# Top-k attention and a dropless expert layer on one core: three experts' rows of the first batch are filled up to whole blocks with empty rows, and 27 blocks instead of 26 are dealt during attention

## The chip, the cores and the metric

The kernel runs on one core of one Trainium2 chip. The metric is the device time of one execution in microseconds (us). Three timed executions of the kernel before gave 1338.06, 1338.33 and 1339.21 us, so the median is 1338.33 us.

## The reference

The first half is attention with a top-k mask, the second an expert layer in which each row goes to one expert only. Cut to what matters:

```python
# q, k, v: (8 batches, 8 heads, 576, 64)
scores = (q @ k^T) / 8
kth = the 32nd largest score of each query row
scores = where(scores >= kth, scores, -1e9)
attn_out = softmax(scores) @ v
x = attn_out as 4608 rows of 512          # 576 rows from each batch
logits = x @ w_gate                       # 8 experts
expert_idx = argmax(logits)
gate_w = softmax(logits)[expert_idx]
for e in range(8):                        # rows of expert e
    y[rows] = relu(x[rows] @ w1[e]) @ w2[e]   # 512 -> 1024 -> 512
return gate_w * y
```

All data is 32-bit floating point. How many rows each expert gets is known only when the kernel runs.

## The kernel before, in words

**Attention.** The work is cut into 144 groups, 18 for each of the 8 batches. A group is two tiles of 128 query rows; a unit is two heads of one batch, and nine groups make two units. One pass of the main loop (`loop`, L1123 on, `i` is the group) issues, for its group: on VectorE a fold of the next group's scores (L306, L308, later L314, L316), a search of the 32 largest values (MAX8 and MATCH_REPLACE8 on L345, L354, L362); on ScalarE `low` (L371), the depth below the threshold (L387) and the exponential (L404); on GpSimd the subtraction between those two (L396); on TensorE the scores of a group four ahead (L292), transposes (L415, L427, L429) and, once per unit, the product with v (L450). The orders of TensorE, ScalarE and VectorE are written out by hand; the queues of SP and GpSimd are laid out by the framework, apart from GpSimd instructions that are chained to each other.

**Dealing blocks.** When the last unit of a batch ends (`ending`, L1012 on), the batch's 576 rows are scattered to a DRAM buffer `x_rows` (L567, five indirect DMAs on GpSimd's queue), where every expert has a range of its own of CAP = 4736 rows. `run` holds the next free row of each expert. Then `table` (L597 to L654, fifteen small VectorE instructions on one partition for a batch) lists full blocks: blocks of 128 rows that no later row can change. How many are listed after each batch is fixed when the program is built, in `new_of`: 0, 4, 4, 5, 4, 5, 4 for the batches 0 to 6, 26 in all. Where `new_of` is 0, no table is made.

**Blocks in the shadow of attention.** A block (`block`, L879 on) loads 257 KB of rows (L749) and 4 MB of weights (L741, L743; two buffers), transposes the rows (L788), multiplies by w1 (L893), applies relu (L898), multiplies by w2 (L910), scales (L919) and puts its rows out with an indirect DMA (L808). Its TensorE work is handed out in 16 pieces: eight of four matmuls on L893, eight of one on L910 (in the trace each matmul is two instructions). A planner in `loop` spends a credit: it grows in each group by `rate` for each of its two tiles, and `rate` is set at group 13 of each batch b from 1 on to `new_of[b - 1] * 16 / 36`. So 4 blocks are spread over the 18 groups that follow at 3.56 pieces a group, 5 blocks at 4.44. In the last five groups of the last batch the credit is spread so that KEEP = 48 pieces, three blocks, are left over. These fill TensorE while the last batch is being finished.

**The end.** After the last batch, `counted` counts each expert's full blocks (a rest of over 64 rows is filled up and counts as full) and its halves (a rest of 1 to 64 rows). A first table gives SURE = 2 blocks, then `end_table` (L669 to L736) gives the rest: HALVES = 4 slots in which a full block and a half of the same expert go through the weights together (`long_block`, 192 rows), and PLAIN = 4 slots of plain blocks. `fill_up` (L582) writes 128 empty rows behind each expert's last row. An empty row has a scale of 0 and an output row number past the end, so that nothing is written for it; the rows come from the tile `blank`. What does not fit the slots is counted in `rest_i`, and a branch behind the main part works it off; another branch repeats everything exactly if a search was in doubt. After attention 3 kept, 2 sure, 4 long and 4 plain blocks follow.

At the start of the program SP's queue loads the first units and then writes one block of empty rows (L942), to which unused slots point.

Of the kernel before, what the change touches and what calls it, by code (L numbers as in the profile page):

```python
# [9 lines left out]
F32 = mybir.dt.float32  # L10
I32 = mybir.dt.int32
AF = mybir.ActivationFunctionType
ALU = mybir.AluOpType
# [24 lines left out]
def _inner(ap: bass.AP, n: int) -> bass.AP:  # L38
    return _ins(ap, len(ap.ap), n)
# [3 lines left out]
def kernel(  # L43
# [47 lines left out]
    nc = tc.nc  # L91
    B, U, P, _ = qk.shape
    N, Dm = out.shape
    S = N // B
    E = moe_w_gate.shape[1]
# [4 lines left out]
    ST = S - SM  # L100
# [7 lines left out]
    FT = F // P  # L108
    XW = Dm + 2
    EB = N // P  # L110
    NSLOT = EB + E - 1
    CAP = N + P
    EMPTY = E * CAP // P
# [1 line left out]
    assert N % P == 0 and TOP_K == 32 and DT == U and P == 2 * D  # L115
    scale = float(D) ** -0.5
    sure = [max(0, -((E * (P - 1) - S * (b + 1)) // P)) for b in range(B - 1)]
    upto_of = [max(0, (S * (b + 1) - E * ST) // P - 1) for b in range(B - 1)]
    upto_of = [max(a, c) if b else 0 for b, (a, c) in enumerate(zip(sure, upto_of))]
    new_of = [b - a for a, b in zip([0] + upto_of, upto_of)]  # L120
    assert all(n >= b - a for n, a, b in zip(new_of, [0] + sure, sure))
    LAST = NSLOT - sure[-1]
    HALVES = E // 2
    SURE = 2
    PLAIN = EB - upto_of[-1] - HALVES - SURE
    LONG = P + ST
    assert PLAIN >= 0 and (N - E * (P - 1) + P - 1) // P - upto_of[-1] >= SURE
    assert LAST - SURE + HALVES <= NSLOT and PLAIN + HALVES <= NSLOT

    k = SimpleNamespace()  # L130
# [25 lines left out]
    const = ctx.enter_context(tc.tile_pool(name="const", bufs=1))  # L156
# [5 lines left out]
    x_rows = dram.tile([(EMPTY + 1) * P, XW], F32, name="x_rows")  # L162
# [16 lines left out]
    for odd in range(2):  # L179
        for h in range(2):  # L180
            r = slice(h * D, (h + 1) * D)
# [16 lines left out]
    e_at = iota_f("e_at", [P, E], [[CAP, E]])  # L198
# [18 lines left out]
    run = const.tile([P, E], F32, name="run")  # L217
    nc.vector.tensor_copy(run, e_at)
    rest_i = const.tile([1, 1], I32, name="rest_i")
    rare = const.tile([1, 1], F32, name="rare")  # L220
    slot_last = const.tile([1, 2, NSLOT], I32, name="slot_last")
    slot_long = slot_last[:, 0, NSLOT - 3 * E:].rearrange("o (i e) -> o i e", i=3)
    assert LAST - SURE <= NSLOT - 3 * E
    done = const.tile([1, E], F32, name="done")
    nc.vector.tensor_scalar_mul(done, e_at[0:1, :], 1.0 / P)
    slot_max = const.tile([1, 2], F32, name="slot_max")
    nc.vector.memset(slot_max[:, 0:1], float(E - 1))
    nc.vector.memset(slot_max[:, 1:2], float(EMPTY))
    upto_all = const.tile([1, E + 1], F32, name="upto_all")
# [7 lines left out]
    blank = const.tile([P, XW], F32, name="blank")  # L237
# [323 lines left out]
    def scattering(r, x):  # L561

        mine = []

        def scatter(i):
            rows_i = slice(0, P if i < NC else ST)
            put = nc.gpsimd.indirect_dma_start(  # L567
                out=x_rows[:, :], out_offset=bass.IndirectOffsetOnAxis(ap=r.posi[rows_i, i:i + 1], axis=0),
                in_=x[rows_i, i, :], in_offset=None,
            ).ins  # L570
            if not k.exact:
                tc.add_manual_dep(put, k.last_pool.name, AFTER)
                for other in mine:
                    tc.declare_no_dep(put, other, reason="the rows of one batch go to different places")
                for other in fetched:
                    tc.declare_no_dep(put, other, reason="new rows go behind all full blocks")
                mine.append(put)
                scattered.append(put)

        return [lambda i=i: scatter(i) for i in range(KC)]  # L580
# [16 lines left out]
    def table(slot_i, n, last, riding=None):  # L597

        sm = k.small
        full = sm.tile([1, E], F32, name="full")  # L600
        ci = sm.tile([1, E], I32, name="ci")
        left = sm.tile([1, E], F32, name="left")
        past = sm.tile([1, NSLOT, E], F32, name="past", bufs=1)
        slot_f = sm.tile([1, 2, NSLOT], F32, name="slot_f", bufs=1)
        upto, step = upto_all, step_all

        def steps():
            if last:
                nc.vector.tensor_scalar_add(full, run[0:1, :], float(P - 1))
                yield  # L610
            nc.vector.tensor_copy(ci, full if last else run[0:1, :])
            yield
            nc.vector.tensor_single_scalar(ci, ci, 7, op=ALU.arith_shift_right)
            yield
            nc.vector.tensor_copy(full, ci)
            yield
            if riding is not None:
                nc.vector.tensor_tensor(full, full, riding, op=ALU.subtract)
                nc.vector.tensor_tensor(full, full, done, op=ALU.max)
                yield  # L620
            nc.vector.tensor_tensor(left, full, done, op=ALU.subtract)
            yield
            nc.vector.tensor_tensor_scan(upto[:, 1:], ones[0:1, 0:E], left, 0.0, op0=ALU.mult, op1=ALU.add)
            yield
            nc.vector.tensor_tensor(step[:, 0:E - 1], done[:, 1:E], full[:, 0:E - 1], op=ALU.subtract)
            yield
            nc.vector.tensor_tensor(
                past[:, 0:n, :], _inner(slots[:, 0:n], E), _ins(upto[:, 1:], 1, n), op=ALU.is_ge
            )
            yield  # L630
            nc.vector.tensor_reduce(slot_f[:, 0, 0:n], past[:, 0:n, :], axis=AX.X, op=ALU.add)
            yield
            nc.vector.tensor_tensor(past[:, 0:n, :], past[:, 0:n, :], _ins(step[:, :], 1, n), op=ALU.mult)
            yield
            nc.vector.tensor_reduce(slot_f[:, 1, 0:n], past[:, 0:n, :], axis=AX.X, op=ALU.add)
            yield
            nc.vector.scalar_tensor_tensor(
                out=slot_f[:, 1, 0:n], in0=slot_f[:, 1, 0:n], scalar=done[:, 0:1], in1=slots[:, 0:n],
                op0=ALU.add, op1=ALU.add,
            )  # L640
            yield
            nc.vector.tensor_tensor(slot_i[:, :, 0:n], slot_f[:, :, 0:n], _inner(slot_max[:, :], n), op=ALU.min)
            yield
            if last:
                nc.vector.tensor_copy(rest_i, upto[:, E:])
            else:
                nc.vector.tensor_scalar_min(upto, upto, float(n))
                yield
                nc.vector.tensor_tensor(left, upto[:, 1:], upto[:, 0:E], op=ALU.subtract)
                yield  # L650
                nc.vector.tensor_tensor(done, done, left, op=ALU.add)
                yield

        return steps()  # L654

    def counted():

# [11 lines left out]
    def end_table(slot_i, slot_l, n, half, full):  # L669
# [16 lines left out]
            v.tensor_scalar(to, to, what[:, 0:1], None, ALU.add)  # L686

        def steps():
            v.tensor_tensor_scan(hupto[:, 1:], ones[0:1, 0:E], half, 0.0, op0=ALU.mult, op1=ALU.add)
            v.tensor_tensor(left, full, done, op=ALU.subtract)  # L690
            v.tensor_scalar(take, hupto[:, 1:], float(HALVES), None, ALU.is_le)
            v.tensor_tensor(take, take, half, op=ALU.mult)
            v.tensor_tensor(take, take, left, op=ALU.min)
# [16 lines left out]
                out=slot_f[:, 1, 0:m], in0=slot_f[:, 1, 0:m], scalar=done[:, 0:1], in1=at[:, 0:m],  # L710
                op0=ALU.add, op1=ALU.add,
            )
            v.tensor_tensor(slot_i[:, :, 0:n], slot_f[:, :, 0:n], _inner(slot_max[:, :], n), op=ALU.min)
            yield
            v.tensor_tensor(past[:, 0:E, :], _inner(slots[:, 0:E], E), _ins(hupto[:, 1:], 1, E), op=ALU.is_ge)
            v.tensor_reduce(long_f[:, 0, :], past[:, 0:E, :], axis=AX.X, op=ALU.add)
# [220 lines left out]
    with fast:  # L937
        units = [(b, u) for b in range(B) for u in range(U)]
        unit.append(load_unit(*units[1]))
        for n in unit:  # L940
            load_values(n)
        nc.sync.dma_start(x_rows[EMPTY * P:(EMPTY + 1) * P, :], blank)  # L942

        work = [(b, g) for b in range(B) for u in range(0, U, 2) for g in groups(u)]
        per_batch = len(work) // B
# [66 lines left out]
        def ending(b, u):  # L1012
# [48 lines left out]
            yield "pool"  # L1061
            through(steps)
            scatters.extend(scattering(r, x))
            if b == B - 1:
                scatter(KC)
                slot_i = k.small.tile([1, 2, NSLOT], I32, name="slot_i")
                half, full = counted()
                through(table(slot_i, SURE, False, half))
                firsts = [(slot_i[0:1, 0, j:j + 1], slot_i[0:1, 1, j:j + 1]) for j in range(SURE)]
                ready = load_rows(SimpleNamespace(), firsts[0][1], True)  # L1070
# [15 lines left out]
            if b == B - 1:  # L1086
                spare.extend(coming[PLAIN:])
                del coming[PLAIN:]
                longs = [[slot_long[0:1, i, j:j + 1] for i in range(3)] for j in range(E)]
                spare.extend((expert, half) for expert, half, _ in longs[HALVES:])  # L1090
                coming[0:0] = [(expert, [full, half]) for expert, half, full in longs[:HALVES]]
                assert len(loaded) == 2 and not waiting
                fill_up()
                coming[0:0] = [(firsts[0][0], ready)] + [(expert, (piece,)) for expert, piece in firsts[1:]]
                scatter(0)
# [126 lines left out]
    with ExitStack() as outer:  # L1222
# [10 lines left out]
        with ExitStack() as st:  # L1233
# [44 lines left out]
                    put()  # L1278
                nc.vector.tensor_scalar_add(ids, ids, S)
            fill_up()  # L1280
            slot_i = slot_last
            for _ in table(slot_i, NSLOT, True):
                pass
            nc.sync.dma_start(slot_d.rearrange("(a n) o -> o a n", a=2), slot_i)
# [53 lines left out]
```

## Time and profile before

| what | value |
|---|---|
| median of three timed executions | 1338.33 us (1338.06 to 1339.21) |
| the profiled execution's own time | 1339.03 us |
| its span, first to last instruction | 1337.4 us |
| TensorE matmul busy | 1189.3 us (89%) |
| VectorE busy | 1076.6 us (81%), 4629 instructions |
| ScalarE busy | 930.8 us (70%) |
| GpSimd busy | 661.9 us (49%) |
| weights loaded | 72 DMAs of 2 MB: 36 blocks |
| mean granted TensorE clock | 0.955 |

The span has two stages that overlap a little. Up to about 1073 us attention runs, and VectorE is busy almost without a gap; blocks are added on TensorE from 367 us on. From then on VectorE has nearly nothing to do, and TensorE works through the remaining blocks. Two things help in reading the rows. A busy share near 100% says that an engine has no gaps, not that its instructions run at their best: VectorE instructions of one line have different lengths in this trace. And a group of the attention loop can be told in the trace by the first fold, L306, which comes once in each of the 144 groups; the time from one to the next is the length of a group, about 7 us.

### The profile page before, as it was taken

The numbers are of one execution on the slowest core, as the hardware profiler recorded it, in microseconds if no ns is written. First come the engines' busy times: TensorE is split into PE (matmuls) and PEld (weight loads), VectorE is DVE, ScalarE is ACT, GpSimd is POOL, SyncE is SP. The second block draws the span as 40 slices with busy tenths as digits, with TensorE's granted clock in tenths as the row PEclk, the third lists the DMA queues.
The fourth block names the chain that finished last, engine by engine and source line by source line (L and its number), as shares of the span: only waits on it lengthen the run. The fifth ranks groups of instructions, "written<-read, shape, count | busy, mean of one in ns | idle before, by whom it ended". The sixth has DMA issues, their size and how long they took to land. (4 is left out here: it accounts for less than half of the span.)

```text
span 1337.4 us, 24295 instructions
## 1 busy us (share of the span) xinstructions
PE 1189.3 (89%) x7570; PEld 831.4 (62%) x7570; DVE 1076.6 (81%) x4629; ACT 930.8 (70%) x2125; POOL 661.9 (49%) x805
## 2 busy tenths in 40 slices
PE   5667766766799999999999999999999999999995
PEld 3344443444466766676677666666677667699973
DVE  7999999999999999999999999999999932000000
ACT  4788788887888888888787888887778851111110
POOL 3454547555755665567555756475547642000000
PEclk9788788888899999999999999999999999999998
DMA  2000001001384348435855294329452739946790
GB/s 84 30 29 30 30 29 65 29 29 38 122 305 168 108 164 288 160 110 175 297 208 179 74 350 170 118 76 372 171 204 87 283 116 332 369 146 219 290 342 18
DMA packets 95563, 214.36 MB, mean 160 GB/s; under 512 B 4926, under 2 KB 25662, under 8 KB 95424
## 3 DMA queue, kind: packets, MB, share of 16 engines
q1 hardware_dynamic: 88800, 192.45, 40.8%
q0 software_dynamic: 6336, 19.97, 4.2%
q8 instruction: 61, 1.00, 0.3%
q14 instruction: 78, 0.64, 0.2%
q10 hardware_dynamic: 288, 0.30, 0.1%
HBM read 191.42 MB, written 21.80 MB: 159 GB/s over the span
## 5 line engine op out<-in xcount | busy, mean ns | idle before, releaser
L396 POOL TENSOR_TENSOR w<-s,w 128x576 f32<-128x576 f32 x288 | 410.2, 1444 | 418.4 <-ACT w L387 418.4
L893 PE MATMUL ph<-xTs,w 128*128 128x128 f32 x2048 | 250.2, 276 | 5.9 <-ACT xTs L790 5.9
L893 PEld LDWEIGHTS ph<-xTs,w 128*128 128x128 f32 x2048 | 239.1, 192 | 21.9 <-issue 14.6
L910 PE MATMUL py<-w,hT 128*128 128x512 f32 x512 | 236.2, 597 | 0.0
L404 ACT ACTIVATE w<-w,nbias 128x576 f32<-128x576 f32 x288 | 224.1, 792 | 3.0 <-POOL w L396 2.0
L292 PE MATMUL sc<-qkb 64*128 64x288 f32 (+1 forms) x1280 | 206.0, 473 | 9.5 <-ACT s L299 5.1
L387 ACT ACTIVATE w<-s,low 128x576 f32<-128x576 f32 x288 | 207.6, 768 | 4.7
L415 PE MATMUL wTm<-turn,w 128*128 128x128 f32 x1152 | 170.1, 287 | 32.0 <-ACT xl L468 21.4
L415 PEld LDWEIGHTS wTm<-turn,w 128*128 128x128 f32 x1152 | 132.0, 145 | 92.5 <-issue 34.4
L299 ACT COPY s<-sc 128x576 f32<-128x576 f32 x288 | 168.9, 640 | 10.4 <-PE sc L292 10.4
L1217 DVE CAST any_i<-pd 1x1 int32<-1x1 f32 x1 | 0.1, 145 | 207.9 <-PE pd L1215 207.9
L422 ACT COPY wT<-wTm 128x512 f32<-128x512 f32 x256 | 139.2, 604 | 39.3 <-PE wTm L415 39.2
L354 DVE MAX8 tops<-scr 128x8 f32<-128x168 f32 x576 | 162.8, 317 | 0.0
L450 PE MATMUL po<-wT,vb 128*64 128x288 f32 x1024 | 154.9, 450 | 0.4 <-ACT wTt L437 0.4
L354 DVE MAX8 tops<-few 128x8 f32<-128x144 f32 (+1 forms) x576 | 154.4, 300 | 0.0
L292 PEld LDWEIGHTS sc<-qkb 64*128 64x128 f32 (+1 forms) x1280 | 110.1, 195 | 65.4 <-issue 25.6
L910 PEld LDWEIGHTS py<-w,hT 128*128 128x128 f32 x512 | 90.7, 190 | 90.4 <-issue 89.2
L808 POOL DMA_INDIRECT out_dram<-y,xg x40 | 42.6, 1066 | 189.8 <-ACT y L869 82.5
L345 DVE MAX8 few<-l 128x8 f32<-128x288 f32 x288 | 127.3, 442 | 0.0
L450 PEld LDWEIGHTS po<-wT,vb 128*64 128x64 f32 x1024 | 74.2, 150 | 77.3 <-issue 26.0
L306 DVE TENSOR_TENSOR h<-s 128x576 f32<-128x576 f32 x144 | 114.8, 797 | 3.9 <-ACT s L299 3.7
L308 DVE TENSOR_TENSOR l<-s 128x576 f32<-128x576 f32 x144 | 108.0, 750 | 0.0
(175 smaller groups left out, 1649.8 us busy)
## 6 DMA issues: line engine op xcount, KB each, us to landing
w<-in_moe_w_dram SPq DMA_DIRECT2D x72, 2048.0 KB, 8.6
qkb<-in_qk_dram SPq DMA_DIRECT2D x31, 608.0 KB, 5.8
vb<-in_v_dram SPq DMA_DIRECT2D x32, 320.0 KB, 3.1
xg<-x_rows SPq DMA_DIRECT2D x36, 257.0 KB, 10.6
x_rows<-blank SPq DMA_DIRECT2D x5, 257.0 KB
x_rows<-blank POOLq DMA_DIRECT2D x4, 257.0 KB, 8.2
x_rows<-x,posi POOLq DMA_INDIRECT x40, 3.1
out_dram<-y,xg POOLq DMA_INDIRECT x40, 4.5
```

The lines of the kernel that those rows point to most:

```text
L292: nc.tensor.matmul(ps[rows, j, 0:HF], n.q[d, cols], n.k[d, keys], start=True, stop=True)
L299: lambda m=m, ps=ps: nc.scalar.copy(s[:, m, :, :], ps[:, :, 0:HF]) for m, ps in enumerate(got)
L345: nc.vector.max(out=f.few[:, m, QF + 8 * j:QF + 8 * j + 8], in_=away)
L354: nc.vector.max(out=tops[:, m, r * 8:(r + 1) * 8], in_=src[m])
L387: nc.scalar.activation(w[:, m, :], s[:, m, :, :].rearrange("p j k -> p (j k)"), AF.Relu, scale=-STEEP, bias=low[:, m:m + 1],)
L396: k.last_pool = in_turn(nc.gpsimd.tensor_tensor(w[:, m, :], s[:, m, :, :].rearrange("p j k -> p (j k)"), w[:, m, :], op=ALU.subtract)).ins
L404: nc.scalar.activation(w[:, m, :], w[:, m, :], AF.Exp, scale=scale, bias=nbias[:, m:m + 1], accum_out=n.z[:, c:c + 1])
L415: nc.tensor.transpose(pm[:, c * P:(c + 1) * P], w[:, m, first:first + P], ident)
L422: nc.scalar.copy(wT[:, :, m, q], pm4)
L450: nc.tensor.matmul(po[r, 0:HF], n.v[:, c, r], rhs, start=(c == 0), stop=(c == KC - 1))
L893: nc.tensor.matmul(ph[:, f, :], n.w1[:, 0, dt, fc * P:(fc + 1) * P], n.xT[:, dt, :], start=(dt == 0), stop=(dt == DT - 1),)
L910: nc.tensor.matmul(py, hT[:, f, :], n.w2[:, 0, f, :], start=(f == 0), stop=(f == FT - 1))
```

## The change

The rows of batch 0 no longer wait for batch 1. Behind batch 0, a new function picks the three experts with most rows (at least as many as the third largest count) and moves their `run` on to 128, so that each of them has one full block:

```python
def filled_up():
    most, few = k.small.tile([P, E], F32, name="left"), k.small.tile([P, E], F32, name="full")
    nc.vector.tensor_tensor(few, run, e_at, op=ALU.subtract)
    nc.vector.max(out=most, in_=few)
    nc.vector.tensor_scalar(few, few, most[:, SOON - 1:SOON], float(P), ALU.is_ge, ALU.mult)
    nc.vector.tensor_tensor(few, few, e_at, op=ALU.add)
    nc.vector.tensor_tensor(run, run, few, op=ALU.max)
```

The rows between the batch's own and 128 are empty ones, which the start of the program writes at the head of each expert's range. The dealing changes to 3, 2, 4, 5, 4, 5, 4 blocks, 27 in all, so that a table is made behind batch 0 too and the first blocks are handed out from group 31 on (batch 1, group 13) instead of group 49. At the end, `end_table` turns a half whose expert has no full block left to go with it into a plain block. The diff, without the changes that only resize tables or move a tile:

```diff
+    SOON = 3
-    upto_of = [max(0, (S * (b + 1) - E * ST) // P - 1) for b in range(B - 1)]
-    upto_of = [max(a, c) if b else 0 for b, (a, c) in enumerate(zip(sure, upto_of))]
+    upto_of = [(S * (b + 1) - E * ST) // P for b in range(B - 1)]
+    upto_of = [max(a, c) if b else SOON for b, (a, c) in enumerate(zip(sure, upto_of))]
-    LAST = NSLOT - sure[-1]
+    LAST = NSLOT + SOON - sure[-1]
-    PLAIN = EB - upto_of[-1] - HALVES - SURE
+    PLAIN = EB - upto_of[-1] - HALVES - SURE + 1
...
         def steps():
+            v.tensor_tensor(left, full, done, op=ALU.subtract)
+            v.tensor_tensor(some, half, left, op=ALU.subtract)
+            v.tensor_scalar_max(some, some, 0.0)
+            v.tensor_tensor(half, half, some, op=ALU.subtract)
+            v.tensor_tensor(full, full, some, op=ALU.add)
+            v.tensor_tensor(left, left, some, op=ALU.add)
+            yield
             v.tensor_tensor_scan(hupto[:, 1:], ones[0:1, 0:E], half, 0.0, op0=ALU.mult, op1=ALU.add)
-            v.tensor_tensor(left, full, done, op=ALU.subtract)
...
-        nc.sync.dma_start(x_rows[EMPTY * P:(EMPTY + 1) * P, :], blank)
+        for r in [e * CAP for e in range(E)] + [EMPTY * P]:
+            nc.sync.dma_start(x_rows[r:r + P, :], blank)
...
             through(steps)
             scatters.extend(scattering(r, x))
+            if b == 0:
+                filled_up()
```

PLAIN stays 4 (36 - 26 - 4 - 2 before, 36 - 27 - 4 - 2 + 1 after); the last listing grows from 17 to 20 slots, and the three more go to the branch that works off what does not fit. SURE, HALVES, KEEP and the planner are as before.

More of the change, by code (lines that the diff above doesn't have):

```diff
@@ L117 @@
     sure = [max(0, -((E * (P - 1) - S * (b + 1)) // P)) for b in range(B - 1)]
-    upto_of = [max(0, (S * (b + 1) - E * ST) // P - 1) for b in range(B - 1)]
-    upto_of = [max(a, c) if b else 0 for b, (a, c) in enumerate(zip(sure, upto_of))]
+    upto_of = [(S * (b + 1) - E * ST) // P for b in range(B - 1)]
+    upto_of = [max(a, c) if b else SOON for b, (a, c) in enumerate(zip(sure, upto_of))]
     new_of = [b - a for a, b in zip([0] + upto_of, upto_of)]
     assert all(n >= b - a for n, a, b in zip(new_of, [0] + sure, sure))
-    LAST = NSLOT - sure[-1]
+    LAST = NSLOT + SOON - sure[-1]
     HALVES = E // 2
     SURE = 2
-    PLAIN = EB - upto_of[-1] - HALVES - SURE
+    PLAIN = EB - upto_of[-1] - HALVES - SURE + 1
     LONG = P + ST
-    assert PLAIN >= 0 and (N - E * (P - 1) + P - 1) // P - upto_of[-1] >= SURE
+    assert PLAIN >= 0 and E == 8 and SOON < E
     assert LAST - SURE + HALVES <= NSLOT and PLAIN + HALVES <= NSLOT
@@ L219 @@
     rest_i = const.tile([1, 1], I32, name="rest_i")
[L220 to L223, printed above, removed]
+    slot_last = const.tile([1, 2, NSLOT + SOON], I32, name="slot_last")
+    slot_long = slot_last[:, 0, NSLOT + SOON - 3 * E:].rearrange("o (i e) -> o i e", i=3)
+    assert LAST - SURE <= NSLOT + SOON - 3 * E
     done = const.tile([1, E], F32, name="done")
     nc.vector.tensor_scalar_mul(done, e_at[0:1, :], 1.0 / P)
-    slot_max = const.tile([1, 2], F32, name="slot_max")
+    slot_max = const.tile([1, 3], F32, name="slot_max")
+    rare = slot_max[:, 2:3]
     nc.vector.memset(slot_max[:, 0:1], float(E - 1))
@@ L641, in steps @@
             yield
-            nc.vector.tensor_tensor(slot_i[:, :, 0:n], slot_f[:, :, 0:n], _inner(slot_max[:, :], n), op=ALU.min)
+            nc.vector.tensor_tensor(slot_i[:, :, 0:n], slot_f[:, :, 0:n], _inner(slot_max[:, 0:2], n), op=ALU.min)
             yield
@@ L712, in steps @@
             )
-            v.tensor_tensor(slot_i[:, :, 0:n], slot_f[:, :, 0:n], _inner(slot_max[:, :], n), op=ALU.min)
+            v.tensor_tensor(slot_i[:, :, 0:n], slot_f[:, :, 0:n], _inner(slot_max[:, 0:2], n), op=ALU.min)
             yield
@@ L1091, in ending @@
                 coming[0:0] = [(expert, [full, half]) for expert, half, full in longs[:HALVES]]
-                assert len(loaded) == 2 and not waiting
+                assert len(loaded) == 2
                 fill_up()
@@ L1280 @@
             fill_up()
-            slot_i = slot_last
+            slot_i = slot_last[:, :, 0:NSLOT]
             for _ in table(slot_i, NSLOT, True):
```

## The prediction

> **What bounds the kernel now.** First the page's 40 slices of 33.4 us, to see which engine is full where.
>
> ```profile
> PE   5667766766799999999999999999999999999995
> DVE  7999999999999999999999999999999932000000
> PEclk9788788888899999999999999999999999999998
> ```
>
> VectorE (DVE) is full until slice 32, some 1073 us, TensorE (PE) from slice 11 to the end. So there are three stages: VectorE alone, both, TensorE alone. Next I cut the span where blocks arrive, 18 groups to a row (by the first folds, L306; the first block matmul is near 367.5), and read the busy times.
>
> ```profile
> core 0: us, PE busy (x) PEld busy (x) DVE busy (x) ACT busy (x) POOL busy (x), PEclk, DMA share, GB/s
> 109.70:238.30 128.60, 90.64 (x538) 54.20 (x536) 128.00 (x557) 105.23 (x246) 74.58 (x93) 0.85 0.12 40
> 238.30:367.50 129.20, 92.15 (x554) 55.91 (x552) 129.20 (x572) 104.93 (x246) 74.40 (x93) 0.86 0.17 55
> 367.50:498.00 130.50, 126.21 (x856) 87.79 (x854) 130.50 (x573) 112.20 (x258) 78.45 (x96) 1.00 0.52 181
> 498.00:630.40 132.40, 129.12 (x876) 89.35 (x874) 132.06 (x572) 113.54 (x264) 80.94 (x97) 1.00 0.51 182
> 630.40:773.10 142.70, 140.99 (x951) 98.30 (x948) 139.34 (x573) 114.03 (x265) 87.63 (x98) 1.00 0.57 201
> 773.10:907.60 134.50, 131.22 (x887) 90.60 (x887) 133.37 (x572) 115.24 (x265) 82.52 (x97) 1.00 0.51 179
> 907.60:1050.30 142.70, 140.99 (x951) 98.33 (x948) 139.32 (x573) 114.05 (x264) 87.59 (x98) 1.00 0.55 196
> 1072.80:1137.00 64.20, 61.16 (x362) 43.52 (x362) 19.76 (x111) 21.54 (x51) 20.27 (x27) 0.97 0.71 232
> ```
>
> I call the rows 0, 1, A, B, C, D, E. Rows 0 and 1 have no block: 18 groups take 129 us, VectorE without a gap. Row A carries 4 blocks (the same cut for L893 and L910 has 256 and 62 instructions, that is 32 + 31 of 64 pieces) and takes only 1.3 us more. B and D also carry 4 and take 3.2 and 5.3 us more, C and E carry 5 and take 13.5 us more. **Four blocks to 18 groups are nearly free, a fifth is not.** The last row is the end of attention: TensorE is busy 61 of 64 us there. The end of the whole span is blocks in a row; on GpSimd the last two output DMAs, one a block, are 14.0 us apart:
>
> ```profile
> 1308.94 0.97 POOL L808 DMA_INDIRECT out_dram<-y,xg  x1 [13.48 <-ACT y L919]
> 1322.95 0.97 POOL L808 DMA_INDIRECT out_dram<-y,xg  x1 [13.04 <-ACT y L919]
> ```
>
> **What becomes of the blocks.** I worked the planner's rule through by hand, group by group. Before: 64, 64, 80, 64, 80 pieces from groups 49, 67, 85, 103, 121, then 16 more. After: 48 from group 31, 32 from group 49, and from group 67 on the same 64, 80, 64, 80, 16, group for group, with 49 pieces left after the loop both times. Then 3 kept, 2 sure, 4 long, 4 plain. So the end, and rows B to E, have the same plan; the 27th block is done in attention. What differs is rows 0, 1 and A: 0, 0, 4 blocks become 0, 3, 2.
>
> Does the data fit the slots? I counted the experts' rows from the reference's inputs. Batch 0 gives 103, 79, 74, 60, 96, 61, 55, 48; experts 0, 1 and 4 are filled up with 25 + 49 + 32 = 106 empty rows. The deals of 3, 2, 4, 5, 4, 5, 4 then all find full blocks. At the end 36 full blocks and 5 halves stand where 36 and 4 stood; one half (expert 1) has no partner, becomes a plain block, and 27 + 2 + 4 + 4 = 37 slots hold all. Nothing goes to the branch behind.
>
> **Part by part.**
>
> *A table behind batch 0.* Fifteen small instructions, one at a time between the search's. In batch 2 the groups that hold one start at 316.94, 324.81 and end at 332.23; the same two groups of batch 1, without one, run 188.98, 195.90, 203.04. 15.29 less 14.06 is **+1.23 us**, on VectorE and so on the path. Bounds: 15 x 0.15 (a row such as L615) = 2.3 above; 0.6 below, if half of it goes into gaps.
>
> *`filled_up`.* Five dependent instructions of 128x8 on VectorE behind a search. Four of their kind, L514 to L520 on 128x40, start at 1098.67 and end at 1099.33: 0.165 each, so **+0.8 us**. Below: 5 x 0.08 (1.23 / 15) = 0.4. Above: one of them meets GpSimd's L396, as L613 does here, 1.21 for 0.17 us:
>
> ```profile
> 321.17 0.17 DVE L613 TENSOR_SCALAR ci<-ci 1x8 int32<-1x8 int32 x1
> ...
> 450.54 1.21 DVE L613 TENSOR_SCALAR ci<-ci 1x8 int32<-1x8 int32 x1
> ```
>
> ```profile
> 448.93 2.79 POOL L396 TENSOR_TENSOR w<-s,w 128x576 f32<-128x576 f32 x2 [3.96 <-ACT w L387]
> ```
>
> so 1.9 us. I take 0.8, as L396 ends 3 us ahead of the end of a group in row 0 (190.19 + 2.84 for a group from 188.98 to 195.90). The Trainium skill (GPSIMD Engine Reference, 8. Key points) says that GpSimd shares SBUF interfaces with VectorE, against VectorE instructions with two SBUF inputs or in a 2-port mode; by it three of the five could meet GpSimd, 3 us, but only if they fall beside it.
>
> *Three blocks in row 1.* By A's row, which is 4 blocks in the same cold start, between 0 and 1.3; I take **+0.3**. Upper bound, if row 1 behaves like D: 5.3 x 3/4 = 4.0.
>
> *Two blocks in A instead of four.* A's largest excess is L613's 1.04 us above, in a group with TensorE full. With half of the pieces I take that it goes, **-1.0**; bounds -1.3 and +1.4 (D's 5.3 x 2/4 - 1.3).
>
> *B to E.* Same plan, entered with less behind: 0, at best B becomes A, -1.9.
>
> *Eight more writes of empty rows at the start.* 8 x 0.36 us (L942) of SP's time from 9.35 us on and 2.06 MB, at 209 to 345 GB/s as in the first microseconds some 6 to 10 us. SP's next DMA is a qkb load at 22.47 us, whose first matmul is at 56.74. So 0; were the queue held 30 us longer, VectorE would wait. The scatters of batch 0 come near 200 us.
>
> *`end_table`.* Five more links, some 1.0 us, between 1106.6 and 1114 us. `fill_up`'s writes behind it wait for the scatters until 1117.3 anyway, SP's next weight load is at 1123.7, and TensorE has the kept blocks: 0, at most 1.0. The 27th block's DMAs (one L749, L741, L743 on SP, one L808 of 1.04 us on GpSimd) fall into rows 1 and A, where the DMA share was 0.17 and 0.52: 0.
>
> Sum: 1.23 + 0.8 + 0.3 - 1.0 = **+1.3 us**. On the profiled execution's own 1339.03 us (span 1337.4 and 1.6 around it) that is 1340.3. It lies 0.7 above the median, so the prediction is 1338.33 + 1.3 = **1339.6 us**.
>
> The clock is a rule against the change. Rows 0 and 1 have 0.85 and 0.86, row A has 1.00; row 1 after lies between. The Trainium skill (TensorE: Matmul & The Clock Gate, What's actually happening) has the array at half rate after an idle window of about 3.4 us, and at full rate only after a busy one. Spread thinner, by that rule, three blocks of 14.0 us at 0.85 would make 92 + 49 = 141 us of TensorE work in 129, +12 us; by row A, where 63 pieces raised the clock at once, nothing.
>
> **The rivals.**
>
> 1. *The blocks push GpSimd's subtraction into the second fold* (slower). In row 0 L396 ends 1.7 us before L314 starts (193.03, 194.69). Once ScalarE is over 1.7 us late they meet: in row C L314 and L316 at 698.66 take 1.40 and 1.66 for 0.44 and 0.45 us, +2.2 a time. For it: B and D, same plan, 3.2 and 5.3. Against it: A. Price: 1.23 + 0.8 + 4.0 + 1.4 = +7.4, 1345.7 us; half of it 1342.
>
> 2. *A cleaner entry* (faster). B behaves as A and A as row 1: 1.23 + 0.8 - 1.3 - 1.9 = -1.2, 1337.2 us. It would take another 1.5 us from C to pass the measurement's limit.
>
> 3. *The change doesn't do what it says:* the 27th block isn't absorbed and is left at the end, 14.0 + 2.0, 1354.3 us. The worked plan speaks against it.
>
> **How the numbers follow.** About 0.2% (2.7 us, so under 1335.7 or over 1341.0) is what a measurement can tell from no change. The forecast has 0.55, rival 2 0.17, rival 1 0.25, rival 3 0.03. The forecast's own range is 1338.4 to 1341.0. Rival 2 lies in no change but for 0.06 that passes 1335.7. Of rival 1 about 0.22 lies over 1341, with rival 3 0.25. So faster 0.06, no change 0.69, slower 0.25. The range cuts 0.06 below 1336.6 and some 0.14 above 1344.0.
>
> **What would show it.** In the profile after: L893 starts near 238 us; L613 occurs eight times, the first near 193 us; VectorE's groups 18 by 18 take about 130.6 (row 0, with table and `filled_up`), 129.5, 129.5, and then B to E unchanged; 74 weight loads, and from the last fold to the end the same time. Wrong if L314 and L316 grow beside L396 in rows 1 and A, if TensorE's clock stays at 0.85 there, if VectorE waits for s before 60 us, or if more than 49 pieces are left after the loop.

## The result, and the profile after

The changed kernel takes 1341.18 us (median of 11; 1339.65 to 1343.12) where the kernel before took 1338.92 us in the same series (median of 11; 1337.48 to 1339.44). The ratio is 1.0020 with a 95% interval of 1.0011 to 1.0029: 2.3 us slower (1.5 to 3.9), at the edge of what was called no change. The forecast was 1.3 us. The profiled execution took 1340.06 us, with a span of 1338.4, only 1.0 us over the span of before. Why one execution shows less than the medians is part of what follows.

The first of the views shown of before, the 40 slices of the page, now of the kernel after:

```profile
PE   5667767898988889999999999999999999999995
DVE  7999999999999999999999999999999942000000
PEclk9788887999998989999999999999999999999998
```

The blocks begin four slices earlier: counted from 0, TensorE is near 80 or 90% from slice 7 on, where it was at 60 or 70. Its clock rises with them, but falls back in slices 12 and 14, in the stretch with two blocks. VectorE stays full. Then the same rows of 18 groups, cut at the first folds as before, in the order 0, 1, A, B, C, D, E, end of attention:

```profile
core 0: us, PE busy (x) PEld busy (x) DVE busy (x) ACT busy (x) POOL busy (x), PEclk, DMA share, GB/s
108.90:240.50 131.60, 94.99 (x544) 57.08 (x542) 131.37 (x578) 104.99 (x246) 75.41 (x93) 0.82 0.17 54
240.50:370.80 130.30, 118.88 (x800) 79.64 (x798) 130.30 (x573) 110.99 (x257) 79.43 (x95) 0.98 0.41 145
370.80:501.10 130.30, 108.07 (x698) 70.08 (x695) 129.50 (x572) 108.93 (x254) 76.67 (x95) 0.93 0.31 109
501.10:632.60 131.50, 128.24 (x870) 89.00 (x868) 131.16 (x572) 112.64 (x259) 80.78 (x97) 1.00 0.52 185
632.60:775.30 142.70, 140.99 (x950) 98.32 (x949) 139.33 (x573) 114.01 (x265) 87.58 (x98) 1.00 0.55 199
775.30:909.80 134.50, 131.24 (x887) 90.61 (x887) 133.39 (x572) 115.26 (x266) 82.57 (x97) 1.00 0.52 181
909.80:1052.50 142.70, 140.99 (x950) 98.31 (x949) 139.36 (x573) 114.03 (x265) 87.61 (x98) 1.00 0.55 198
1075.00:1139.20 64.20, 61.16 (x366) 43.55 (x365) 20.47 (x116) 21.51 (x51) 20.30 (x27) 1.00 0.74 243
```

Read against the rows of before: row 0 grew from 128.60 to 131.60, row 1 from 129.20 to 130.30, A stayed (130.50, 130.30), B shrank from 132.40 to 131.50, and C, D and E have the same lengths. To the hundredth, with the first folds' own times, the ledger of the two executions is: the 15 groups ahead of row 0 -0.91, row 0 +2.95, row 1 +1.08, A -0.12, B -0.98, C to E 0.00, from the last fold to the end -1.13, and +0.13 at the start. That is the +1.0 of the spans.

Three of these terms have nothing to do with the change. Ahead of row 0 one group (66.4 us) is 0.8 shorter, and it is so in every one of the seven other kernels below, the variants of before too. In row 0 another one (144.9 us) is 0.5 shorter; in the seven it comes out either like before or 0.7 shorter. And in the end of attention the kernel before had one stretch of half clock that the profile after has not:

```profile
1089.80:1093.20 3.40, 3.40 (x16) 1.75 (x18) 0.22 (x1) 0.54 (x4) 0.00 (x0) 0.50 0.00 0
```

It holds 16 matmuls in 3.4 us at a granted clock of 0.50, and from the last fold the first block after it comes out 1.7 us later than in the profile after. Three of the variants of after below have such a stretch there too, and the two variants of before have none, so it doesn't go with the change. Together the three terms make 2.6 us between these two executions. Left out, the profile says +2.95 + 0.5 + 1.08 - 0.12 - 0.98 + 0.13 = 3.6 us, and the interval of the medians reaches to 3.9. But the profiled execution of before took about its kernel's median (1339.03 us, the median is 1338.92), and that of after 1.1 us less than its own. So 3.6 is the ledger of one pair of executions, and the medians' 2.3 stays the measure of the loss.

### The profile page after: what moved, and what is told of

Read it like the earlier page. It is cut to its first block, busy times and chain, and to the rows that moved or that the text cites. A ratio compares the mean times of both kernels' runs of the same rounds, so it can differ in the third digit from the quotient of the medians.

```text
span 1338.4 us, 24522 instructions
## 1 busy us (share of the span) xinstructions
PE 1199.8 (90%) x7654; PEld 839.9 (63%) x7654; DVE 1079.0 (81%) x4654; ACT 932.5 (70%) x2129; POOL 666.0 (50%) x806
## 5 line engine op out<-in xcount | busy, mean ns | idle before, releaser
L397 POOL TENSOR_TENSOR w<-s,w 128x576 f32<-128x576 f32 x288 | 411.4, 1448 | 415.9 <-ACT w L388 415.9
L909 PE MATMUL ph<-xTs,w 128*128 128x128 f32 x2112 | 259.2, 277 | 7.0 <-ACT xTs L806 7.0
L909 PEld LDWEIGHTS ph<-xTs,w 128*128 128x128 f32 x2112 | 247.0, 192 | 25.0 <-issue 16.4
L926 PE MATMUL py<-w,hT 128*128 128x512 f32 x528 | 245.5, 597 | 1.4 <-ACT hT L914 1.4
L293 PE MATMUL sc<-qkb 64*128 64x288 f32 (+1 forms) x1280 | 203.1, 468 | 9.6 <-ACT s L300 5.1
L309 DVE TENSOR_TENSOR l<-s 128x576 f32<-128x576 f32 x144 | 109.2, 758 | 0.0
```

Source lines behind the costliest of these rows:

```text
L293: nc.tensor.matmul(ps[rows, j, 0:HF], n.q[d, cols], n.k[d, keys], start=True, stop=True)
L397: k.last_pool = in_turn(nc.gpsimd.tensor_tensor(w[:, m, :], s[:, m, :, :].rearrange("p j k -> p (j k)"), w[:, m, :], op=ALU.subtract)).ins
L909: nc.tensor.matmul(ph[:, f, :], n.w1[:, 0, dt, fc * P:(fc + 1) * P], n.xT[:, dt, :], start=(dt == 0), stop=(dt == DT - 1),)
L926: nc.tensor.matmul(py, hT[:, f, :], n.w2[:, 0, f, :], start=(f == 0), stop=(f == FT - 1))
```

## The experiments

Theory 1 says that the loss is made by the few instructions behind batch 0: `filled_up` takes its own time on VectorE and pushes the next fold beside GpSimd's subtraction, and the table adds its time; the blocks themselves cost little, but the early start brings nothing, because from group 67 on just as many blocks are left as before. The rival, theory 2, puts the loss into the blocks of rows 1 and A and their lower clock.

### The five instructions, spread out

```diff
 def filled_up():
     nc.vector.tensor_tensor(few, run, e_at, op=ALU.subtract)
+    yield
...
-                filled_up()
+                aside.append(filled_up())
```

A `yield` follows each of the five, so that they are handed out one at a time between the instructions of the search.

> filled_up's five instructions are handed out one at a time between the instructions of the search, as the table's are, instead of in a row behind it. Theory 1 (the five in a row cost their own 0.93 us and push the next fold, L309, beside GpSimd's subtraction L397, 1.96 us for 0.75): the five cost about 0.4 us and L309 is back at 0.75, so 1.5 to 1.9 us less than the kernel after, +0.4 to +0.8 us over before by the medians. Theory 2 (the loss is in the blocks of the first two stages and their clock): at most 0.5 us less than after, +1.7 us over before.

Measured: 1339.70 us, ratio 1.0011 (1.0002 to 1.0020), where the kernel after has 1.0020. In the kernel before, the second fold and the subtraction on GpSimd in the group that matters:

```profile
189.64 0.75 DVE L308 TENSOR_TENSOR l<-s 128x576 f32<-128x576 f32 x1
```

```profile
190.19 2.84 POOL L396 TENSOR_TENSOR w<-s,w 128x576 f32<-128x576 f32 x2 [4.34 <-ACT w L387]
```

In the kernel after, the timeline of VectorE and that of GpSimd (lines are numbered one higher there, so these are L309 and L397):

```profile
187.69 0.14 DVE L660 TENSOR_TENSOR full<-run,e_at 128x8 f32<-128x8 f32 x1
...
188.54 0.17 DVE L664 TENSOR_TENSOR run<-run,full 128x8 f32<-128x8 f32 x1
188.62 0.75 DVE L307 TENSOR_TENSOR h<-s 128x576 f32<-128x576 f32 x1
189.29 1.96 DVE L309 TENSOR_TENSOR l<-s 128x576 f32<-128x576 f32 x1
```

```profile
188.90 3.63 POOL L397 TENSOR_TENSOR w<-s,w 128x576 f32<-128x576 f32 x2 [4.34 <-ACT w L388]
```

The five take 0.93 us (187.69 to 188.62). The subtraction on GpSimd waits for ScalarE, not for them, so it begins where it did, 8.72 us after the first fold of the group ahead (181.47 to 190.19 in before, 180.18 to 188.90 here). The fold L309, which now comes later than that, runs into it: 1.96 us for 0.75, and the two subtractions take 3.63 us for 2.84. With the five spread out:

```profile
187.43 0.73 DVE L307 TENSOR_TENSOR h<-s 128x576 f32<-128x576 f32 x1
188.09 0.74 DVE L309 TENSOR_TENSOR l<-s 128x576 f32<-128x576 f32 x1
191.24 0.26 DVE L660 TENSOR_TENSOR full<-run,e_at 128x8 f32<-128x8 f32 x1
```

L309 is back at 0.74, as theory 1 expects. But the gain is smaller than the 1.5 to 1.9 that I wrote: some 1.2 us by the two ratios, whose intervals overlap, and 0.5 in the rows. Row 0 is 1.07 us shorter than after (0.2 of it in the group at 144.9 us named above). The table comes later, with ten of its fifteen instructions in the second of its two groups instead of five, and one of them (L648) meets another GpSimd instruction, 0.95 us for 0.15. Row 1 is 0.56 longer, where L614 of the next table takes 1.20 us.

### `filled_up` twice

```diff
             if b == 0:
                 filled_up()
+                filled_up()
```

> filled_up is called twice in a row; the second call changes nothing in run. Theory 1: the folds behind it start another 0.9 us later, so that both L307 and L309 lie beside L397: 1.6 to 2.3 us more than the kernel after in the groups around 190 us. Rival (each instruction costs its own time and no more): 0.9 us more. Elsewhere both expect nothing but a different draw of the clock's windows.

Measured: 1344.00 us, ratio 1.0038 (1.0024 to 1.0051). Row 0 takes 134.04 us; the groups that start at 181.5 and 189.0 in before are 4.9 us longer than there, and 2.0 longer than after. That is the size of theory 1, not the 0.9 of the rival. The instructions that met were others than I expected:

```profile
189.52 0.17 DVE L661 MAX8 left<-full 128x8 f32<-128x8 f32 x1
189.72 1.19 DVE L662 TENSOR_SCALAR full<-full,left 128x8 f32<-128x8 f32 x1
190.95 1.33 DVE L663 TENSOR_TENSOR full<-full,e_at 128x8 f32<-128x8 f32 x1
192.31 0.17 DVE L664 TENSOR_TENSOR run<-run,full 128x8 f32<-128x8 f32 x1
192.40 0.75 DVE L307 TENSOR_TENSOR h<-s 128x576 f32<-128x576 f32 x1
```

GpSimd's two subtractions run from 189.47 to 192.26. Two tiny instructions of the second call come while they run and take 1.19 and 1.33 us for 0.2, and each ends when a subtraction ends (190.91 beside 190.89, 192.28 beside 192.26); the folds behind them find GpSimd free and are as short as ever. So the price isn't set by the size of the instruction that is late. Nor does every instruction pay it: L661, the MAX8 of the second call, runs beside the first subtraction in its usual time.

### The same 27 blocks, started at group 49

```diff
-rate = new_of[b - 1] * PIECES / (U * NT)
+rate = [0, 5, 4, 5, 4, 5, 4][b - 1] * PIECES / (U * NT)
```

> The kernel after, but the planner gives no rate before group 49 and then five blocks in the 18 groups from 49 on. Theory 1 (the early start is what makes the 27th block cheap; five blocks in 18 groups cost 13.5 us wherever they are): groups 31 to 48 get about 1 us shorter, groups 49 to 66 about 11 to 13 us longer, 10 to 12 us over the kernel after, ratio to before about 1.009. Rival (the first stage with blocks starts cold and would take five as well as four): 0 to 2 us over the kernel after.

Measured: 1352.92 us, ratio 1.0109 (1.0094 to 1.0125), 11.7 us over the kernel after. Rows 1, A and B:

```profile
241.07:370.38 129.31, 92.46 (x540) 55.40 (x538) 129.18 (x572) 104.66 (x246) 74.18 (x93) 0.84 0.27 95
370.38:511.83 141.45, 139.54 (x941) 97.73 (x938) 135.79 (x572) 112.69 (x258) 83.18 (x97) 1.00 0.43 149
511.83:646.24 134.41, 131.51 (x887) 90.62 (x887) 133.30 (x572) 115.18 (x266) 82.56 (x97) 1.00 0.50 179
```

Row 1 is 1.0 shorter than after, A 11.1 longer, B 2.9 longer. The rival falls: a cold start doesn't take five blocks as well as four. So the early start does what it should, as it takes 48 pieces for about 1 us; but the change spends it on a block that the kernel before doesn't have. The four groups of row 0 that hold `filled_up` and the table are together 3.46 us longer than in before, exactly as in after, though no block follows them before group 49. Theory 2 is left with row 1's 1.0 us.

### Even rates, on the kernel before and on the kernel after

```diff
-rate = new_of[b - 1] * PIECES / (U * NT)
+rate = [0, 4, 4, 4.5, 4.5, 4.75, 4][b - 1] * PIECES / (U * NT)
```

> The kernel before with the planner's rates made even: 4, 4, 4.5, 4.5, 4.75 blocks instead of 4, 4, 5, 4, 5 in the stages from group 49 on (21 instead of 16 pieces fall into the last five groups). Theory 1 (a stage takes four blocks nearly free and pays for the fifth, so that uneven rates lose): the two stages of 142.7 us get 5 to 7 us shorter each, the one of 134.5 us 1 to 3 us longer, the last groups 1 to 2 us longer: 6 to 10 us less than before, ratio 0.993 to 0.9955. Rival (the cost goes by the pieces in all, wherever they are): within 2 us of before.

Measured: 1335.87 us, ratio 0.9981 (0.9972 to 0.9990), 2.6 us less than before. Rows C, D and E:

```profile
629.64:768.24 138.60, 136.16 (x934) 95.41 (x934) 137.94 (x573) 116.21 (x268) 83.14 (x97) 1.00 0.59 211
768.24:904.73 136.49, 134.38 (x895) 92.36 (x896) 134.82 (x572) 112.98 (x261) 84.67 (x99) 1.00 0.50 175
904.73:1046.00 141.27, 139.47 (x956) 98.20 (x954) 138.29 (x573) 117.08 (x270) 86.29 (x98) 1.00 0.53 192
```

C is 4.1 shorter, D 1.9 longer, E 1.4 shorter with 74 pieces for 79. The direction is that of theory 1, the size less than half of the 6 to 10 us that I expected. The profile's span says -4.6, the medians -2.6 (1.3 to 3.7 by the interval). The rival's 2 us lie inside that, so it is the rows, and not the medians, that speak against it.

The kernel after with the five spread out and rates of 3, 2, 4, 4.5, 4.5, 4.75:

> The kernel after with filled_up handed out piece by piece and the planner's rates made even: 3, 2, 4, 4.5, 4.5, 4.75 blocks. Theory 1 (the early start gives nothing as long as 19 blocks are still left behind group 67, as in the kernel before): the same gain as the even rates gave the kernel before, 2 to 5 us, on a kernel that is 1 to 1.5 us slower, so 0 to 2 us above the kernel before with even rates, about 1337. Rival (the early start leaves room that even rates can use): below the kernel before with even rates.

Measured: 1337.18 us, ratio 0.9992 (0.9983 to 1.0001). That lies 1.3 above the kernel before with even rates, as theory 1 expects; rows C, D and E are 138.61, 136.58 and 141.17, the same within 0.1. The two intervals overlap, so the rows carry this again: the early start alone gives even rates nothing to work with.

### One block fewer at the end

```diff
+    upto_of = [3, 6, 10, 15, 19, 24, 28]
-    SURE = 2
+    SURE = 1
-rate = new_of[b - 1] * PIECES / (U * NT)
+rate = [3, 3, 4, 4.4, 4.4, 4.6, 4][b - 1] * PIECES / (U * NT)
```

This is the kernel after, with the five spread out, that deals as many blocks as these inputs have full in time; PLAIN stays 4, and 12 blocks follow attention. The numbers dealt are fitted to these inputs; no other inputs were run.

> As after_even, but 28 blocks are dealt (3, 3, 4, 5, 4, 5, 4, which these inputs have full in time) and SURE is 1, so that the end has 12 blocks after attention instead of 13 and attention one more, in groups 49 to 66 and in even rates of 3, 3, 4, 4.4, 4.4, 4.6. Theory 1 (room on TensorE before group 67 is nearly free, and a block at the end costs 14.0 us): the end gets 13 to 14 us shorter, groups 49 to 66 0 to 2 us longer, the rest 0 to 3 us longer: 9 to 13 us less than after_even, ratio to before 0.989 to 0.993. Rival (the end's blocks hide the last batch's work, which then shows): the end gets less than 8 us shorter.

The same step on the kernel before, without the early start (0, 5, 4, 5, 4, 5, 4 blocks, rates of 4.4, 4.4, 4.5, 4.5, 4.7 from group 49 on):

> The kernel before with the same step: 27 blocks dealt (0, 5, 4, 5, 4, 5, 4), SURE 1, 12 blocks after attention, even rates of 4.4, 4.4, 4.5, 4.5, 4.7 from group 49 on. Theory 1 (without the early start the block taken from the end goes into stages that are full): the end 13 to 14 us shorter, the two stages from group 49 to 84 together 6 to 10 us longer, so 3 to 7 us less than the kernel before with even rates, and 5 to 8 us above after_more. Rival (the early start is of no use even then): within 2 us of after_more.

Measured: 1323.86 us, ratio 0.9883 (0.9868 to 0.9898), against 1333.64 us, 0.9966 (0.9954 to 0.9979). With the early start it is 13.3 us less than after_even, a little more than the 9 to 13 expected, and 14.2 less than before: **the version that beats both kernels**. Without it the step brings 2.2 us over the even rates, less than the 3 to 7 I expected, and stays 9.8 over the version with it, more than the 5 to 8. Rows 1, A and B with the early start, then A and B without:

```profile
239.67:370.71 131.04, 119.95 (x804) 81.03 (x802) 131.04 (x573) 110.71 (x257) 80.92 (x95) 0.98 0.41 143
370.71:501.58 130.87, 119.32 (x794) 80.42 (x792) 130.87 (x572) 111.51 (x258) 80.48 (x96) 0.97 0.41 146
501.58:632.63 131.05, 126.81 (x858) 88.11 (x856) 130.72 (x572) 112.61 (x259) 81.21 (x97) 1.00 0.52 184
```

```profile
366.65:501.06 134.41, 132.43 (x912) 93.61 (x909) 133.58 (x573) 113.60 (x261) 83.52 (x96) 1.00 0.60 214
501.06:636.84 135.78, 134.71 (x910) 92.95 (x908) 134.42 (x573) 114.00 (x266) 82.32 (x99) 1.00 0.49 170
```

With 3 blocks, then 3, then 4, each of these rows takes 131 us; a third block in A costs 0.8 us over after_even. With 4.3 and 4.4 blocks and no early start, A and B take 134 and 136, together 7.3 more than in before_even, as expected. From the last fold to the end it is 264.2 us, 10.1 less than in after_even (274.3) and not 13 to 14; before_more has 261.3, 11.6 less than before_even. TensorE enters that stretch further behind (the last groups have 26 pieces for 21), so part of the block's 14 us is probably given back there; I have not separated it further. The rival, under 8 us, falls. The step also lowers the rates, from 4.5, 4.5 and 4.75 to 4.4, 4.4 and 4.6, and rows C to E are 4.7 us shorter than in after_even, so not all of the gain comes from the end.

## Why the prediction was right or wrong, point by point

- **The plan from group 67 on** was right, and it is the reason for the whole result: rows C, D and E agree to 0.01 us, 74 weight loads were made, nothing went to the branch behind. Those are 37 blocks instead of 36, as the rows filled up make one more in all. The change moves that one through rows that were nearly free, and gains nothing anywhere.
- **The table, +1.23,** was right: the four groups of row 0 that grew add up to 3.46 us, and 0.93 of `filled_up` and 1.21 of L309 leave 1.3. That is a remainder; no run took the table alone away.
- **`filled_up`, +0.8,** is the step that failed: "I take 0.8, as L396 ends 3 us ahead of the end of a group". The five are clear of the subtraction, as it says, and took 0.93 us. But they stand in front of the next group's folds, and the next subtraction doesn't wait for them. The step asked whom the new instructions meet, and not whom they make late: L308 ended at 190.39 in before, 0.2 us after the subtraction began at 190.19. The term was 2.1 us, outside my upper bound of 1.9.
- **Three blocks in row 1, +0.3,** measured 1.08; within its bounds. One L513 of a choice (1.36 us for about 0.2) and one L612 of a table (0.73 for 0.25) stretched there.
- **Two blocks in A, -1.0,** measured -0.12. What I expected came: the group with L613 is 1.06 shorter. But TensorE's clock fell to half in between:

```profile
401.90:408.70 6.80, 5.73 (x23) 3.01 (x25) 6.80 (x31) 4.83 (x12) 3.04 (x5) 0.50 0.00 0
```

```profile
410.69 0.22 DVE L480 RECIPROCAL rz<-rz 128x10 f32<-128x10 f32 x1 [0.80 <-ACT rz L476]
```

  TensorE is late, ScalarE behind it, and VectorE waits 0.80 us in a group that is 0.9 longer. In the experiments the same group is 0.93 and 0.69 us longer where a slow stretch of 6.8 us lies there (`filled_up` spread out, and with even rates on top), and not longer with `filled_up` twice, where the only one near ends as the group begins (409.8 and 409.6 us). So the clock did speak against thinly spread blocks, for about 1 us where the whole rule would have made 12: the row's mean is 0.93, row 1 has 0.98. The Trainium skill (TensorE: Matmul & The Clock Gate, What's actually happening) names a half-rate state after idle windows of about 3.4 us. The two stretches of 0.50 shown here last 3.4 and 6.8 us, which agrees with it in length. But TensorE was not wholly idle ahead of them: of the 3.4 us before, it was busy for 1.69 ahead of the first and 0.67 ahead of the second.
- **B, 0 to -1.9,** measured -0.98: half of rival 2. The groups at 511.9 to 526.5 us are 0.96 shorter together; the plan there is the same, and I take it that TensorE enters with less behind, which I have not shown.
- **The writes at the start and the longer `end_table`,** both 0: the first fold is 0.13 us later, and the last stretch isn't longer. Right.
- **Rival 1** did not come as described: L314 and L316 did not stretch together in rows 1 and A. Its mechanism, a VectorE instruction beside GpSimd's subtraction, came at another place. **Rival 3** did not come.
- **The sum:** 1.3 was forecast, 2.3 (1.5 to 3.9) measured. `filled_up` missed 1.3, row 1 0.8 and A 0.9, B gave 1.0 back; with 0.1 each for the table and the start that makes 3.5, the 3.6 of the ledger without the three terms that the change doesn't touch, and inside the interval. That the total came within 1 us of the forecast is in part luck: the three misses add up to 3.0, and B gave a third of it back. Why the medians show 2.3 and not 3.5 stays open. Over the 11 executions of after the time moves with the mean granted clock: 1339.79 us at 0.960, 1343.12 at 0.953. Which of the two leads I have not tested, and the executions of before show no such tie (1337.69 us at 0.948, 1339.46 at 0.955).

## What to carry to other kernels

Ask of a block of work that is started early what is still left at the point where the old plan begins: where the same amount is left, no time is won, however free the early room was. And when short instructions are put in front of others on a full engine, look at whom they delay, and at what the other engines do by then: those keep their own time, and the delayed instruction meets them. Where a stage takes four units nearly free and pays for the fifth, fill the free room first and keep the rest even, and only then take work from the stretch in which nothing hides it.

## What the runs showed of the hardware that I had not expected

- A VectorE instruction of 128x8 that comes while a subtraction runs on GpSimd can last until that subtraction ends: L662 and L663 took 1.19 and 1.33 us instead of 0.23 and 0.17, beside runs of 1.4 us. A MAX8 of the same size (L661, 0.17 us) did not. The Trainium skill (GPSIMD Engine Reference, 8. Key points) names contention for VectorE instructions with two SBUF inputs or in a 2-port mode. L309 and L663 have two inputs, which agrees; L613 and L662 have one tensor, and no row here shows their mode. L661, which was not delayed, has one tensor too.
- Single stretches of half clock come at different places from execution to execution. One of 3.4 us followed a stretch in which TensorE was busy for 1.69 of 3.4 us, and made the first block after the last fold 1.7 us late. In the profile after, the same place is as idle (1.69 of 3.4 us busy from 1088.6 us on) and no slow stretch follows. Two profiles of 1338 us can differ by 1 to 2 us for that alone.
- Where the same plan is entered with the same backlog, the rows of 18 attention groups repeat to 0.02 us over 400 us: rows C to E in before, in after and in the two variants that change only `filled_up`. That makes a ledger by groups possible where medians leave 2 us open.
